# Linear attention and a gated feed-forward layer: attention of chunks 2 to 5 as 64x64 tiles of the array

## The chip, the core and the metric

The kernel runs on one core of a Trainium2 chip. The time is microseconds of the device for one execution. A core has five engines with a queue each, which run their instructions in order and wait for one another by semaphores: TensorE (PE, the matrix array of 128 rows and 128 columns, with its weight loads listed as PEld), VectorE (DVE), ScalarE (ACT), GpSimd (POOL) and SyncE (SP, used here to issue transfers). Results of PE go to PSUM, of which there are eight banks; everything else lives in SBUF.

## The reference

```python
def _attn_ref(q, k, v):                       # 4 batches, 8 heads, 768 tokens, 64 channels
    gamma = 1.0 - 2.0 ** (-5.0 - np.arange(H))
    scale = 1.0 / np.sqrt(D)
    for t in range(S):
        state = gamma[None, :, None, None] * state + np.einsum('bhd,bhe->bhde', k[:, :, t], v[:, :, t])
        y[:, :, t] = scale * np.einsum('bhd,bhde->bhe', q[:, :, t], state)
    return y
def _moe_ref(x, w_gate, w_val, w_out, rms_g): # x: 3072 tokens x 512, d_ff 1536
    rms = np.sqrt(np.mean(x * x, axis=-1, keepdims=True) + 1e-06)
    xn = x / rms * rms_g
    g = xn @ w_gate
    silu = g * (1.0 / (1.0 + np.exp(-g)))
    val = xn @ w_val
    return (silu * val @ w_out)
```

Each head keeps a decaying state of 64x64; a token adds the outer product of its key and value to it and reads it with its query. The eight heads of a token, side by side, are the 512 channels of the second function, which normalises them and runs a gated feed-forward layer. Inputs and output are float32.

## The kernel before

The 768 tokens of a batch are cut into 6 chunks (c) of 128. Inside a chunk attention is computed in the usual parallel form: scores of all pairs of the chunk's tokens, masked so that a query sees only earlier keys, times the values; to that is added what the queries read from the state as it stood before the chunk. Then the chunk's keys and values are added to the state. The decay is put into scale factors on q, k and v, so that from chunk 2 on the mask is only ones and zeros and the state is a plain sum.

The whole kernel is one list, `ORDER`, a string of some 860 words written out ahead. Each word is an operation, the indices of its chunk and batch, the PSUM banks that it uses (behind "/") and, where there is a choice, the engine (behind "@": D, A, P, S). A loop at the end of the kernel (L626 on) goes through the words and calls the function of that name; so the list sets the order of every engine's queue, the order of transfers on each queue among them. There is no other scheduler. Words that matter here, with the lines of the profile:

- `Lq`, `Lk`, `Lv` load q, k, v of a chunk and batch (L331; on POOL a transfer that also casts to bfloat16, on SP a plain one). `Cq` and `V` scale and cast q and v (L359, L378). `tq`, `tk` are transposing transfers on SP that give qT and kT (L407): two heads of 64 channels on the 128 partitions, 128 tokens, four pairs of heads (`hp`).
- `A` (L423): scores. For each pair of heads, two matmuls with 64 rows (the channels of one head) and 128 columns; the two heads stand in the two row halves of the array and write to two banks. One word does two batches.
- `M0`, `M1` (L445): the mask, on DVE, one bank of 128x512 each, from PSUM to bfloat16 in SBUF. Two for each chunk and batch.
- `Y` (L460, L464): masked scores times v, one full-array matmul of 64 columns for each head, and the read of the state, one full-array matmul of 128 columns for each pair of heads, against a block-diagonal bfloat16 copy of the state, `st_b`. For chunk 4 and half of chunk 5 the state is read by `Z` instead (L436), with 64 rows and 64 columns for one head, two batches sharing two banks, and `Y` adds only the scores' part (L455).
- `K` (L551): keys times values, 128 tokens by 64 channels on one half of the columns for each head; `U` (L560) adds the result to the float32 state `st_f` on DVE; `B` (L567) casts the state into `st_b` on POOL, two instructions for each batch.
- `S`, `R`, `N` (L474 to L505): sum of squares on ACT, 1/rms on POOL, the normalised rows on DVE. `XE` (L524): from chunk 2 on a transposing transfer on SP into `xnT`, which holds the four batches of one chunk; before that PE transposes (`X`, L518) and a copy.
- `g`, `v` (L575): gate and value matmuls, one group of 128 of the 1536 hidden channels for all 512 tokens of a chunk being four matmuls of 512 columns. `s` (L586): silu on ACT. `h` (L594): the product on DVE, into `hT`.
- `d` (L601): the output matmuls, 512 columns, twelve for each chunk and batch, in one to three words; `e` (L623) the same for the last tile in three column pieces. `o` (L141) copies to SBUF, `st` (L614) stores from SP's queue.

So a chunk's attention lies on all engines, and the feed-forward groups of the chunk before it (and the output matmuls of the one before that) are put between its steps on PE.

```python
    for w in ORDER.split():
        w, _, now["gate"] = w.partition(">")
        w, _, bk = w.partition("/")
        w, _, en = w.partition("@")
        f, *a = w.split(".")
        last[w] = F[f](ENG.get(en), [int(i) for i in bk], *map(int, a))
```

Of the kernel before, what the change touches and what calls it, by code (L numbers as in the profile page):

```python
# [9 lines left out]
F32 = mybir.dt.float32  # L10
BF16 = mybir.dt.bfloat16
# [23 lines left out]
M1.1.1 d.0.0.0.4/4 Lk.2.0@P s.0.6.7.0.4 h.0.8.9.0.4 d.0.1.0.4/1 h.0.6.7.0.4 Lk.3.1@P M0.1.0 d.0.2.0.4/2 M0.1.1
Tk.1.3/5 Tk.1.2/7 D.1.3@D Ek.1.3@A d.0.3.0.4/6 D.1.2@D Lk.2.1@P Ek.1.2@A A.1.3/53 A.1.2/70 M0.1.3 d.0.2.4.8 M1.1.3
Lk.2.2@P d.0.3.4.8 M1.1.2 Lk.2.3@P M0.1.2 d.0.1.4.8 Lk.3.0@P Y.1.2/7 K.1.1/0 S.1.2 K.1.2.2/3 U.1.1@D K.1.0/5 d.0.0.4.8
U.1.2.2@D R.1.2 U.1.0@D Y.1.0/3 B.1.2 N.1.2 Y.1.1/5 S.1.0 B.1.0 Y.1.3/0 Lq.2.3@S S.1.1 X.1.2/7 R.1.0 d.0.1.8.12
Lq.2.1@S S.1.3 Lq.2.0@S R.1.1 N.1.0 d.0.2.8.12 XE.1.2@A Lv.2.2@S o.0.1@A Lq.2.2@S R.1.3 N.1.1 X.1.0/3 Lv.2.1@S o.0.2@A
d.0.3.8.12 B.1.1 Lv.2.0@S N.1.3 XE.1.0@A X.1.1/2 B.1.3 o.0.3@D d.0.0.8.12 tk.2.2 XE.1.1@A g.1.0.1.0.3/2 o.0.0@A  # L40
v.1.0.1.0.3/6 s.1.0.1.0.3 g.1.2.3.0.3/4 h.1.0.1.0.3 v.1.1.2.0.3/2 g.1.3.4.0.3/6 tk.2.0 v.1.3.4.0.3/0 s.1.3.4.0.3
X.1.3/3 h.1.3.4.0.3 v.1.2.3.0.3/6 XE.1.3@A Cq.2.0@D g.1.1.2.0.3/0 s.1.1.2.0.3 s.1.2.3.0.3 Cq.2.3@D h.1.2.3.0.3
Cq.2.1@D v.1.10.11.0.4/3 g.1.7.8.0.4/0 g.1.10.11.0.4/6 g.1.5.6.0.4/4 g.1.9.10.0.4/5 v.1.5.6.0.4/1 v.1.9.10.0.4/7
tk.2.3 tk.2.1 tq.2.0 tq.2.1 Cq.2.2@P h.1.1.2.0.3 Lq.3.1@S Lq.3.0@S V.2.0@P tq.2.3 tq.2.2 s.1.10.11.0.4 s.1.9.10.0.4
s.1.5.6.0.4 h.1.5.6.0.4 h.1.10.11.0.4 h.1.9.10.0.4 v.1.11.12.0.4/4 g.1.6.7.0.4/1 g.1.11.12.0.4/7 g.1.8.9.0.4/3
v.1.8.9.0.4/5 v.1.7.8.0.4/6 Cq.3.1@P s.1.7.8.0.4 s.1.11.12.0.4 s.1.8.9.0.4 Cq.3.0@P h.1.11.12.0.4 h.1.7.8.0.4
h.1.8.9.0.4 A.2.0/3470 g.1.4.5.0.4/2 v.1.4.5.0.4/6 v.1.6.7.0.4/5 Lv.2.3@S tq.3.1 Lk.3.2@P s.1.6.7.0.4 s.1.4.5.0.4
M0.2.1 M1.2.1 M1.2.0 h.1.6.7.0.4 M0.2.0 V.2.1@P g.1.0.4.3.4/0 A.2.2/4271 v.1.0.4.3.4/5 Y.2.1/3 s.1.0.4.3.4 S.2.1
tk.3.1 V.2.2@P h.1.4.5.0.4 M0.2.2 M0.2.3 h.1.0.4.3.4 M1.2.3 M1.2.2 Lk.3.3@P V.2.3@P tq.3.0 R.2.1 Lv.3.1@S d.1.1.0.10/4
K.2.1/1 K.2.2.2/2 K.2.0/5 Y.2.2/7 Y.2.3/6 Y.2.0/0 d.1.1.10.12 S.2.2 S.2.3 o.1.1@A S.2.0 R.2.2 tk.3.0 N.2.1 U.2.2.2@D  # L50
U.2.0@D U.2.1@D N.2.2 XE.2.1@S R.2.0 Lq.3.3@S XE.2.2@S B.2.1 N.2.0 XE.2.0@S R.2.3 V.3.1@D N.2.3 XE.2.3@S d.1.3.0.12/1
d.1.0.0.10/7 A.3.0/6045 d.1.2.0.12/2 d.1.0.10.12 M0.3.0 M1.3.0 M1.3.1 o.1.3@D M0.3.1 st.0.0@S st.0.3@S B.2.3
v.2.6.7.0.4/1 v.2.1.2.0.4/4 g.2.3.4.0.4/5 g.2.6.7.0.4/0 g.2.1.2.0.4/6 v.2.3.4.0.4/3 Lk.4.1@P s.2.3.4.0.4 o.1.0@A
s.2.6.7.0.4 s.2.1.2.0.4 Lv.3.3@S Lq.3.2@S Cq.3.3@P B.2.0 tq.3.3 Lv.3.0@S tk.3.3 Lv.3.2@S o.1.2@D h.2.6.7.0.4
h.2.3.4.0.4 h.2.1.2.0.4 V.3.0@D Cq.3.2@P v.2.8.9.0.4/6 g.2.8.9.0.4/1 v.2.5.6.0.4/4 g.2.5.6.0.4/3 g.2.7.8.0.4/0 Y.3.0/7
g.2.2.3.0.4/5 g.2.4.5.0.4/2 Lv.4.2@S tq.3.2 Lq.4.2@S s.2.8.9.0.4 S.3.0 s.2.5.6.0.4 s.2.2.3.0.4 g.2.0.1.0.4/3
v.2.2.3.0.4/5 tk.3.2 V.3.3@P V.3.2@D h.2.8.9.0.4 h.2.5.6.0.4 h.2.2.3.0.4 st.1.3@S Lk.4.2@P Lv.4.0@S Lv.5.2@S B.2.2
R.3.0 s.2.7.8.0.4 s.2.4.5.0.4 s.2.0.1.0.4 A.3.2/2046 v.2.4.5.0.4/1 v.2.7.8.0.4/5 v.2.0.1.0.4/3 M0.3.2 M1.3.3 M1.3.2
M0.3.3 h.2.4.5.0.4 h.2.0.1.0.4 N.3.0 h.2.7.8.0.4 Lk.5.0@P Y.3.1/0 Y.3.2/4 g.2.10.11.0.4/1 Y.3.3/3 g.2.9.10.0.4/7
v.2.10.11.0.4/5 v.2.9.10.0.4/6 g.2.11.12.0.4/2 tk.4.1 Cq.4.2@P S.3.1 S.3.2 S.3.3 s.2.9.10.0.4 s.2.10.11.0.4  # L60
s.2.11.12.0.4 st.1.0@S V.4.0@P Lq.4.3@S Lq.4.1@S R.3.1 v.2.11.12.0.4/1 R.3.2 Lv.5.1@S R.3.3 N.3.2 N.3.1 N.3.3
h.2.9.10.0.4 h.2.11.12.0.4 h.2.10.11.0.4 XE.3.0@S d.2.1.0.10/2 d.2.2.0.12/5 K.3.2.2/1 K.3.0.2/6 d.2.1.10.12 Lk.4.0@P
XE.3.2@S XE.3.1@S Lv.4.3@S XE.3.3@S o.2.2@D U.3.0.2@D o.2.1@D U.3.2.2@D v.3.1.2.0.4/5 g.3.9.10.0.4/6 g.3.1.2.0.4/1
g.3.5.6.0.4/2 v.3.5.6.0.4/3 g.3.0.1.0.4/0 v.3.0.1.0.4/7 Lq.4.0@S st.0.2@S st.0.1@S Lk.4.3@P Lv.5.0@S st.1.1@S B.3.1
tk.4.2 Cq.4.3@P s.3.0.1.0.4 s.3.5.6.0.4 s.3.1.2.0.4 Lq.5.3@S h.3.0.1.0.4 h.3.1.2.0.4 Cq.4.1@D h.3.5.6.0.4
v.3.2.3.0.4/0 g.3.3.4.0.4/2 g.3.2.3.0.4/5 v.3.4.5.0.4/1 g.3.4.5.0.4/3 v.3.3.4.0.4/7 g.3.6.7.0.4/4 s.3.2.3.0.4
s.3.3.4.0.4 s.3.4.5.0.4 B.3.2 tq.4.2 V.4.3@P Lq.5.2@S V.4.2@P Cq.4.0@P tq.4.0 h.3.4.5.0.4 h.3.3.4.0.4 h.3.2.3.0.4
Lk.5.1@P tk.4.0 V.5.2@P tq.4.1 B.3.0 s.3.9.10.0.4 s.3.6.7.0.4 Lk.5.2@P Lk.5.3@P B.3.3 tq.4.3 Lv.4.1@S v.3.9.10.0.4/1
v.3.6.7.0.4/6 A.4.0/4073 Z.4.0/25 h.3.9.10.0.4 M0.4.0 h.3.6.7.0.4 Cq.5.2@D M0.4.1 M1.4.0 M1.4.1 Lq.5.0@S Lq.5.1@S
Lv.5.3@S tk.4.3 v.3.8.9.0.4/1 g.3.7.8.0.4/4 v.3.10.11.0.4/6 g.3.10.11.0.4/7 Y.4.0.2 g.3.8.9.0.4/3 d.2.3.0.12/0 V.5.1@P  # L70
# [27 lines left out]
def kernel(  # L98
# [564 lines left out]
```

## Time and profile before

| | |
|---|---|
| median of 3 runs | 231.4 us (231.13 to 231.41) |
| the profiled execution, its own time | 231.01 us |
| its span, first to last instruction or transfer | 229.0 us |
| PE busy | 222.0 us (97%), 1833 matmuls |
| PEld / DVE / ACT / POOL busy | 117.8 / 125.6 / 82.4 / 103.9 us |
| granted TensorE clock | 1.0 |
| transfers | 31.50 MB, mean 138 GB/s |

The page gives each engine's busy time, then the span in 40 slices with one digit each (9 is busy for 90% or more), then the chain of work that ended last. A group of instructions is told as line, engine, operation, tiles, shape and count, then busy time, mean length in ns, and the idle time before them with what ended it. For a matmul the shape tells the tile: 64\*128 is 64 rows by 128 columns of the array, and 64x128 behind it the channels and the columns that move through. A matmul's recorded length includes the way through the array, which the next one overlaps; and a few records can be missing.

### The profile page before, as it was taken

The page shows a single profiled execution, that of the slowest core. Times are in us where ns is not written, and L with a number is a line of the kernel's source. Part 1 is how long each engine was busy: PE and PEld are TensorE (multiplying, and loading weights), DVE is VectorE, ACT ScalarE, POOL GpSimd, SP SyncE. Part 2 cuts the span into 40 slices and gives each one's busy share as a digit, 9 for nine tenths or more (in the row PEclk, how much of TensorE's full clock was granted, in tenths as well). Part 3 has the DMA queues.
Part 4 walks back from the last instruction along what each step waited for, and adds up shares of the span by engine and source line. Part 5 has one row for each costly group of instructions (what it writes and reads, how often), then busy time and mean ns, then how long its engine had stood idle before and what let it go on. Part 6 is the DMA issues. An engine that isn't in the chain of part 4 may idle for free.

```text
span 229.0 us, 4721 instructions
## 1 busy us (share of the span) xinstructions
PE 222.0 (97%) x1833; PEld 117.8 (51%) x1859; DVE 125.6 (55%) x235; ACT 82.4 (36%) x190; POOL 103.9 (45%) x175
## 2 busy tenths in 40 slices
PE   7999999999999999999999999999999999999994
PEld 2677755565544764445544445545554444444642
DVE  6596467955636966357733585956466432163101
ACT  7897142246333240333600525400473322123031
POOL 8999999655408547345708934383130000000000
PEclk9999999999999999999999999999999999999999
DMA  7999999999859957999899997436103620010026
GB/s 146 177 174 185 185 189 190 177 167 194 181 129 157 152 95 133 213 180 283 164 179 288 127 168 155 118 71 139 47 0 69 219 82 0 0 49 0 0 94 227
DMA packets 105351, 31.50 MB, mean 138 GB/s; under 512 B 94449, under 2 KB 102385, under 8 KB 105330
## 3 DMA queue, kind: packets, MB, share of 16 engines
q0 software_dynamic: 40112, 9.70, 46.4%
q1 hardware_dynamic: 65218, 21.51, 42.7%
q8 instruction: 14, 0.23, 0.4%
q14 instruction: 7, 0.06, 0.1%
HBM read 28.31 MB, written 6.29 MB: 151 GB/s over the span
## 4 chain that ended last, share of the span: by engine, by line
PE 86%; DMA 5%; ACT 2%; issue 2%; POOL 1%; SPq 1%; DVE 1%; ACTq 0%; POOLq 0%
PE o_ps L601 25%; PE g_ps L575 25%; PE v_ps L575 24%; PE a_ps L423 3%; DMA xnT<-xn 3%; DMA qb<-in_q_dram 2%; PE y_ps L460 2%; PE kv_ps L551 1%; PE o_ps L623 1%; PE t_ps L386 1%; PE y_ps L464 1%; PE xt_ps L518 1%; SPq L524 1%; PE t_ps L391 1%; ACT sg L586 1%
## 5 line engine op out<-in xcount | busy, mean ns | idle before, releaser
L594 DVE TENSOR_TENSOR hT<-sg,v_ps 128x512 bf16<-128x512 bf16 (+2 forms) x76 | 48.1, 655 | 59.9 <-ACT sg L586 35.8
L586 ACT ACTIVATE sg<-g_ps 128x512 bf16<-128x512 f32 (+2 forms) x76 | 41.8, 575 | 102.5 <-PE g_ps L575 92.9
L575 PE MATMUL v_ps<-xnT,wv_b 128*128 128x512 bf16 (+2 forms) x338 | 70.2, 344 | 0.4
L575 PE MATMUL g_ps<-xnT,wg_b 128*128 128x512 bf16 (+2 forms) x335 | 69.4, 344 | 0.4
L601 PE MATMUL o_ps<-wo_b,hT 128*128 128x512 bf16 x265 | 61.8, 379 | 0.8 <-issue 0.3
L575 PEld LDWEIGHTS <-wv_b 128*128 128x128 bf16 x344 | 30.7, 98 | 30.3 <-issue 0.9
L575 PEld LDWEIGHTS <-wg_b 128*128 128x128 bf16 x344 | 30.3, 98 | 29.8 <-DVE hT L594 0.6
L601 PEld LDWEIGHTS <-hT 128*128 128x128 bf16 x276 | 26.2, 98 | 29.7
L445 DVE TENSOR_TENSOR am<-a_ps,causal 128x512 bf16<-128x512 f32 x32 | 20.3, 683 | 5.0 <-PE a_ps L423 5.0
L567 POOL CAST st_b<-st_f 64x256 bf16<-64x256 f32 x40 | 16.9, 422 | 9.6 <-DVE st_f L560 6.9
L331 POOL DMA_DIRECT2D kb<-in_k_dram x20 | 18.3, 915 | 2.2 <-DMA wo_b<-in_moe_w_out_dram 1.1
L359 POOL TENSOR_TENSOR qb<-qf,ydec 128x512 bf16<-128x512 f32 x10 | 10.4, 1041 | 16.8 <-DMA qf<-in_q_dram 11.3
L141 DVE COPY o_sb<-o_ps 128x512 f32<-128x512 f32 (+1 forms) x11 | 7.2, 658 | 17.5 <-DMA out_dram<-o_sb 11.7
L505 DVE SCALAR_TENSOR_TENSOR xn<-y_ps,rstd,g_bc 128x512 bf16<-128x512 f32 x18 | 13.3, 748 | 5.9 <-POOL rstd L493 5.6
L477 ACT ACTIVATE xsq<-y_ps 128x512 f32<-128x512 f32 x18 | 10.8, 600 | 15.0 <-PE y_ps L464 14.7
L378 POOL TENSOR_TENSOR vp<-vf,vdec 128x512 bf16<-128x512 f32 x12 | 12.8, 1071 | 5.1 <-DMA vf<-in_v_dram 4.8
L141 ACT COPY o_sb<-o_ps 128x512 f32<-128x512 f32 (+2 forms) x15 | 8.0, 555 | 17.1 <-PE o_ps L601 16.6
L493 POOL TENSOR_TENSOR rstd<-ms,mhalf 128x1 f32<-128x1 f32 x21 | 12.0, 572 | 1.7
L445 DVE TENSOR_TENSOR am<-a_ps,mask 128x512 bf16<-128x512 f32 x16 | 10.3, 684 | 2.3 <-PE a_ps L423 2.2
L491 POOL TENSOR_SCALAR ms<-ssq 128x1 f32<-128x1 f32 x21 | 4.3, 206 | 14.8 <-ACT xsq L477 11.4
L490 POOL TENSOR_TENSOR ssq<-ssq 128x1 f32<-128x1 f32 x6 | 1.2, 193 | 16.8 <-ACT xsq L474 16.8
L423 PE MATMUL a_ps<-qT,kT 64*128 64x128 bf16 x192 | 7.8, 217 | 0.6 <-issue 0.3
(95 smaller groups left out, 168.6 us busy)
## 6 DMA issues: line engine op xcount, KB each, us to landing
out_dram<-o_sb SPq DMA_DIRECT2D x23, 256.0 KB, 2.6
vf<-in_v_dram SPq DMA_DIRECT2D x17, 256.0 KB, 4.3
qf<-in_q_dram SPq DMA_DIRECT2D x16, 256.0 KB, 4.1
kb<-in_k_dram POOLq DMA_DIRECT2D x23, 128.0 KB, 5.6
wo_b<-in_moe_w_out_dram POOLq DMA_DIRECT2D x3, 512.0 KB, 9.3
qb<-in_q_dram POOLq DMA_DIRECT2D x8, 128.0 KB, 5.2
vp<-in_v_dram POOLq DMA_DIRECT2D x7, 128.0 KB, 8.8
wv_b<-in_moe_w_val_dram POOLq DMA_DIRECT2D x3, 256.0 KB, 6.3
```

The costliest lines, as they stand in the source:

```text
L141: return (e.copy if e is ACT else e.tensor_copy)(out, in_)
L331: i = done[n, c, b] = e.dma_start(out=x, in_=rows[n][b, c])
L378: e.tensor_tensor(out=u["vp"], in0=u["vf"], in1=vdec[:, c, :, None].to_broadcast([128, H, D]), op=ALU.mult)
L423: nc.tensor.matmul(u["a"][i][:, hp, :], u["kT"][r, hp, :], u["qT"][r, hp, :], start=True, stop=True)
L445: return DVE.tensor_tensor(out=u["am"][:, i], in0=u["a"][i], in1=m, op=ALU.mult)
L493: return POOL.tensor_tensor(out=u["rstd"], in0=ms, in1=mhalf, op=ALU.pow)
L505: return DVE.scalar_tensor_tensor(out=u["xn"], in0=flat(u["y"]), scalar=u["rstd"], in1=g_bc, op0=ALU.mult, op1=ALU.mult)
L567: POOL.tensor_copy(st_b[b][r, :, i * 64:i * 64 + 64], st_f[b // 2][r, b % 2])
L575: r = nc.tensor.matmul(p[:, (n - n0) * m:(n - n0 + 1) * m], W[w][0][:, s, n * 128:(n + 1) * 128], xnT[c][:, s, b0 * C:b1 * C], start=s == ...
L586: return ACT.activation(sg[:, :cols], done["wg", c, n0, b0][:, :cols], AF.Silu)
L594: return DVE.tensor_tensor(out=hT[c][:, n0:n1, b0 * C:b1 * C], in0=sg, in1=p, op=ALU.mult)
L601: nc.tensor.matmul(o_ps[c, b], hT[c][:, n, b * C:(b + 1) * C], wo_b[:, n, :], start=n == 0, stop=n == NFF - 1)
```

## The change

Attention of chunks 2 to 5 is written anew for a pair of batches together (g = 0: batches 0 and 1; g = 1: batches 2 and 3). The chunk is cut into two halves (s) of 64 tokens; the state is also carried from the first half to the second. All matmuls of it have 64 rows, 64 columns and 64 moving columns.

- `a`: scores inside each half alone, 32 matmuls for a pair of batches, into two banks. `m0`, `m1`: the mask, one bank of 128x512 each for two batches, with a mask of 64x64 (`causal_h`, made once by `ch`).
- `k`: keys times values of each half, 32 matmuls, one bank for each half (chunk 5: 16, the first half alone). `u0` adds the first half's bank to `st_f` and writes `st_m`; `u1` adds the second's and writes `st_f`. `b0`, `b1` cast these to bfloat16, `st_h[g][1]` and `st_h[g][0]`, 128x512 in one instruction.
- `z`: 16 of the state reads; `w`: masked scores times v (32 matmuls) and the other 16 state reads. Bank s holds the rows of half s of both batches, so that a row tile (c, 2g + s) of the feed-forward part now holds two half chunks of two batches; `st` stores it through another view of the output.
- `A`, `Z`, `M`, `Y`, `K`, `U`, `B` stay for chunks 0 and 1; the `B` words of chunk 1 become `b1`.
- The words behind the head of the list stand in a new order, with other banks, and some of the two-way choices of engine (`Cq`, `V`, `D`, `XE`, `o`) change. The count of feed-forward words is the same. The ring of the float32 k tile goes from 4 buffers to 1.

The diff, with most of the list cut:

```diff
-h.1.8.9.0.4 A.2.0/3470 g.1.4.5.0.4/2 v.1.4.5.0.4/6 v.1.6.7.0.4/5 Lv.2.3@S tq.3.1 Lk.3.2@P s.1.6.7.0.4 s.1.4.5.0.4
-M0.2.1 M1.2.1 M1.2.0 h.1.6.7.0.4 M0.2.0 V.2.1@P g.1.0.4.3.4/0 A.2.2/4271 v.1.0.4.3.4/5 Y.2.1/3 s.1.0.4.3.4 S.2.1
...
+v.1.0.1.0.3/5 k.2.0/12 tk.2.0 tk.2.1 s.1.0.1.0.3 s.1.6.7.0.4 s.1.1.2.0.3 h.1.6.7.0.4 u0.2.0 h.1.0.1.0.3 v.1.5.6.0.4/6
...
+u1.2.0 z.2.0/06 k.2.1/74 a.2.0/13 h.1.4.5.0.4 tq.2.2 Lq.3.1@S Lq.3.0@S tq.2.3 tk.2.3 m1.2.0 m0.2.0 Cq.3.0@D u0.2.1
...
+h.1.9.10.0.4 u1.2.1 h.1.11.12.0.4 w.2.0 z.2.1/15 a.2.1/72 S.2.0 S.2.1 Lv.3.0@S tk.3.1 Lv.3.1@S tk.3.0 tq.3.1 Lv.3.3@S
...
+u1.3.1 b1.3.0@A s.2.7.8.0.4 s.2.2.3.0.4 b0.3.1@A s.2.9.10.0.4 v.2.0.1.0.4/4 v.2.7.8.0.4/5 g.2.4.5.0.4/1 z.3.1/32
...
+m0.4.0 m1.4.0 h.3.9.10.0.4 u0.5.1 h.3.8.9.0.4 v.3.7.8.0.4/2 w.4.0 z.4.1/63 a.4.1/05 d.2.0.0.10/1 m0.4.1 h.3.7.8.0.4
+m1.4.1 w.4.1 d.3.1.0.10/5 d.2.0.10.12 d.3.1.10.12 d.3.0.0.10/2 d.3.3.0.12/0 d.3.0.10.12 S.4.0 S.4.1 S.4.2 S.4.3 R.4.0
...
+    HC = C // 2
+    out_h = out.rearrange("(g j c s p) m -> c g s j p m", j=2, c=S // C, s=2, p=HC)
...
-    RING = {"q": 4, "k": 4, "v": 6}
+    RING = {"q": 4, "k": 1, "v": 6}
...
+    st_m = [const.tile([128, 2, NHP, D], F32, name=f"st_m{b}") for b in range(B // 2)]
+    st_h = [[const.tile([128, 2, NHP, D], BF16, name=f"st_h{b}_{s}") for s in range(2)] for b in range(B // 2)]
+    causal_h = const.tile([128, HC], BF16, name="causal_h")
...
+    @op
+    def a(e, bk, c, g):
+        ps = pair[c, g]["a"] = [bank(bk[i], [128, 2, NHP, HC], F32, "a_ps") for i in range(2)]
+        for hp in range(NHP):
+            for j in range(2):
+                u = t[c, 2 * g + j]
+                for i in range(2):
+                    for s in range(2):
+                        nc.tensor.matmul(ps[i][half(s), j, hp, :], u["kT"][half(i), hp, half(s)],
+                                         u["qT"][half(i), hp, half(s)], start=True, stop=True)
...
+    @op
+    def k_(e, bk, c, g):
+        kv = pair[c, g]["kv"] = [bank(x, [128, 2, NHP, D], F32, "kv_ps") for x in bk]
+        for hp in range(NHP):
+            for j in range(2):
+                u = t[c, 2 * g + j]
+                for s in range(len(bk)):
+                    for i in range(2):
+                        nc.tensor.matmul(kv[s][half(i), j, hp, :], u["kb"][half(s), 2 * hp + i, :],
+                                         u["vp"][half(s), 2 * hp + i, :], start=True, stop=True)
...
+        return DVE.tensor_tensor(out=st_m[g], in0=st_f[g], in1=pair[c, g]["kv"][0], op=ALU.add)
...
+        return DVE.tensor_tensor(out=st_f[g], in0=st_m[g], in1=pair[c, g]["kv"][1], op=ALU.add)
...
+    def state(c, g, i, s, hp, start=False, stop=False):
+        for j in range(2):
+            nc.tensor.matmul(pair[c, g]["y"][s][half(j), 2 * hp + i, :], t[c, 2 * g + j]["qT"][half(i), hp, half(s)],
+                             st_h[g][s][half(i), j, hp, :], start=start, stop=stop, skip_group_check=True)
+
+    @op
+    def z(e, bk, c, g):
+        pair[c, g]["y"] = [bank(bk[s], [128, H, D], F32, "y_ps") for s in range(2)]
+        for hp in range(NHP):
+            for i in range(2):
+                state(c, g, i, 1 - i, hp, start=hp == 0)
+
+    @op
+    def w(e, bk, c, g):
+        u = pair[c, g]
+        for h in range(H):
+            for s in range(2):
+                for j in range(2):
+                    nc.tensor.matmul(u["y"][s][half(j), h, :], u["am"][half(s), h % 2, j, h // 2, :],
+                                     t[c, 2 * g + j]["vp"][half(s), h, :], start=False, stop=False, skip_group_check=True)
+        for hp in range(NHP):
+            for i in range(2):
+                state(c, g, i, i, hp, stop=hp == NHP - 1)
...
-        e.dma_start(out=out_v[c, b][:, m], in_=done["o", c, b][:, m])
+        o = out_v[c, b][:, m] if c <= 1 else out_h[c, b // 2, b % 2][:, :, m]
+        e.dma_start(out=o, in_=done["o", c, b][:, m])
```

153 lines of the change are left out of this document (88 added, 65 removed).

## The prediction

> **What bounds the kernel now.** I read the page first: busy shares, the slices, the chain of waits.
>
> ```profile
> PE 222.0 (97%) x1833; PEld 117.8 (51%) x1859; DVE 125.6 (55%) x235; ACT 82.4 (36%) x190; POOL 103.9 (45%) x175
> PE   7999999999999999999999999999999999999994
> PEclk9999999999999999999999999999999999999999
> PE 86%; DMA 5%; ACT 2%; issue 2%; POOL 1%; SPq 1%; DVE 1%; ACTq 0%; POOLq 0%
> ```
>
> TensorE is busy in every slice between the first and the last, at full granted clock, and it is 86% of the chain. A busy PE need not be a PE that never waits, so the next view is the waits of PE alone, complete:
>
> ```profile
> engine line waited for: us in total, times, longest us
> PE hot_ps L224 <- DVE one L148: 1.0, 1, 1.0
> PE t_ps L386 <- DMA qb<-in_q_dram: 0.4, 1, 0.4
> PE a_ps L423 <- issue: 0.3, 1, 0.3
> PE o_ps L601 <- issue: 0.3, 2, 0.2
> PE xt_ps L518 <- DVE xn L505: 0.2, 1, 0.2
> ```
>
> The first two rows are the head; behind it PE stands still for 0.8 us in all. So from the head to the last matmul the time is the length of the PE queue, and what the edit takes from that queue comes off the end, if the new list feeds PE as well as the old one. The other engines matter only as feeders.
>
> **What attention costs on PE now.** The groups of 70 to 170 us (by line and shape) give the counts of chunks 2 to 5:
>
> ```profile
> L423 PE MATMUL a_ps<-qT,kT 64*128 64x128 bf16 x128 | 5.0, 217 | 0.5 <-issue 0.3
> L460 PE MATMUL y_ps<-vp,am 128*128 128x64 bf16 x80 | 4.0, 193 | 0.0
> L464 PE MATMUL y_ps<-st_b,qT 128*128 128x128 bf16 x40 | 3.9, 219 | 0.0
> L551 PE MATMUL kv_ps<-vp,kb 128*64 128x64 bf16 x96 | 2.3, 198 | 0.0
> L455 PE MATMUL y_ps<-vp,am 128*128 128x64 bf16 x48 | 2.1, 193 | 0.0
> L436 PE MATMUL y_ps<-st_b,qT 64*128 64x64 bf16 x48 | 1.2, 190 | 0.0
> ```
>
> A row's busy time includes the pipeline's end behind each group, which the next group overlaps. The price of a group is therefore the time from its first start to the next group's first start, in the timeline of PE. The rate of large matmuls comes from one piece of the chain in order of time (start, length, what); the groups follow from the timeline of PE in three windows (start, length, line, names, shapes, count):
>
> ```profile
> 93.28 2.59 PE g_ps L575 x12
> ```
>
> ```profile
> 133.67 0.81 PE L575 MATMUL v_ps<-xnT,wv_b 128*128 128x512 bf16 x3
> 134.41 0.62 PE L423 MATMUL a_ps<-qT,kT 64*128 64x128 bf16 x16
> 134.87 0.40 PE L436 MATMUL y_ps<-st_b,qT 64*128 64x64 bf16 x16
> 135.20 0.60 PE L575 MATMUL v_ps<-xnT,wv_b 128*128 128x512 bf16 x2
> ...
> 118.69 0.81 PE L601 MATMUL o_ps<-wo_b,hT 128*128 128x512 bf16 x3
> 119.43 0.69 PE L551 MATMUL kv_ps<-vp,kb 128*64 128x64 bf16 x32
> 120.06 0.61 PE L601 MATMUL o_ps<-wo_b,hT 128*128 128x512 bf16 x2
> ...
> 79.81 0.71 PE L551 MATMUL kv_ps<-vp,kb 128*64 128x64 bf16 x32
> 80.45 0.41 PE L460 MATMUL y_ps<-vp,am 128*128 128x64 bf16 x8
> 80.69 0.39 PE L464 MATMUL y_ps<-st_b,qT 128*128 128x128 bf16 x4
> 80.92 0.40 PE L460 MATMUL y_ps<-vp,am 128*128 128x64 bf16 x8
> ```
>
> - Twelve large matmuls take 2.59 us: 0.216 each.
> - *Change of tile shape.* Three of them from 133.67 end at 134.32, but the first scores matmul starts at 134.41; at the update, 118.69 + 0.65 = 119.34 against 119.43. Entering a smaller shape costs about 0.09 us; I take 0.095 for each change, in or out.
> - *Scores (L423, two row tiles):* 16 in 0.46 us, 29 ns each.
> - *State read by row tiles (L436):* 16 in 0.33 less one change: 0.235, 15 ns each.
> - *Update (L551, two column tiles):* 32 in 0.63 less one change: 0.535, that is 16 pairs of 33 ns.
> - *Full array:* eight 64-wide (L460, L455) in 0.235, 29 ns each; four 128-wide (L464) in 0.23.
>
> Two tiles thus do run at once: 15 and 17 ns a matmul against 29 for the same 64 columns in the full array.
>
> Removed: 128 scores, 8 groups of 0.46, 3.7 us; 128 masked products, 16 x 0.235, 3.75; 40 full state reads, 10 x 0.23, 2.3; 48 row-tiled ones, 0.7; 96 updates, 3 x 0.535, 1.6. Together 12.05 us.
>
> **What the new attention costs.** For each chunk and pair of batches the code issues 32 matmuls in a, 32 in k (16 for chunk 5, where one bank is given), 16 in z and 48 in w; over eight such pairs 992, all 64x64 with 64 columns moving. Loops are nested so that four in a row go to four different quarters of the array, and the two row halves to different banks; in chunk 5's k only two quarters alternate. That is 240 fours and 16 pairs, 256 periods.
>
> No four-tile group is in this trace. Bounds: if a four goes as fast as a pair of row tiles (2 x 15, 29 ns), 256 x 29 = 7.4 us; if only two of four overlap, 496 periods x 33 ns = 16.4 us. I take 33 ns a four, 256 x 33 = 8.45 us, because rows split the array in one group above and columns in the other, each pair overlapping fully, and I assume that the two halvings don't hinder each other; the slower of the two periods then sets the four. The matmuls save 12.05 - 8.45 = 3.6 us.
>
> One rule speaks against this. The Trainium skill (TensorE: Matmul & The Clock Gate, "Wait — 56ns, not 53.3ns?") holds that starts of matmuls are never closer than about 25 ns, however few columns move. By it the estimate would be 992 x 25 = 24.8 us, 12.75 us more than now. Against the rule stands the row at 119.43: 32 matmuls in 0.63 us, a change of shape included, are 20 ns each.
>
> **Changes of shape.** I counted stretches in both lists. Before, scores, updates and row-tiled reads of chunks 2 to 5 make 24 changes. After, the 64x64 groups stand in 16 stretches, 32 changes, and chunk 1's update is split in two stretches, 2 more. Ten more at 0.095 is +0.95 us. A change to quarters has no row here; if it costs nothing more than the others +0.95 stands, if double, 32 x 0.095 = 3.0 us on top.
>
> **The feeders.** Rows of DVE, ACT and POOL, the landing of the transposing DMAs of L524, and of the loads of v:
>
> ```profile
> L594 DVE TENSOR_TENSOR hT<-sg,v_ps 128x512 bf16<-128x512 bf16 x64 | 42.1, 683 | 53.3 <-ACT sg L586 33.3 <-PE v_ps L575 18.5 <-remote 1.3
> L445 DVE TENSOR_TENSOR am<-a_ps,causal 128x512 bf16<-128x512 f32 x32 | 20.3, 683 | 5.0 <-PE a_ps L423 5.0
> L560 DVE TENSOR_TENSOR st_f<-st_f,kv_ps 128x512 f32<-128x512 f32 x6 | 4.1, 681 | 0.0
> L141 ACT COPY o_sb<-o_ps 128x512 f32<-128x512 f32 x13 | 7.6, 594 | 16.7 <-PE o_ps L601 16.6
> L567 POOL CAST st_b<-st_f 64x256 bf16<-64x256 f32 x40 | 16.9, 422 | 9.6 <-DVE st_f L560 6.9 <-PE y_ps L436 1.2
> DMA to landing us min/median/max: 2.4/3.1/5.1
> vf<-in_v_dram SPq DMA_DIRECT2D x17, 256.0 KB, 4.3
> ```
>
> Masks fall from 32 to 16 on DVE (-10.9 us busy); state sums rise to 14 (9.5 us), where five of this form and two half as wide stood; 32 of the 40 casts leave POOL (those behind chunks 1 to 4) for 16 copies of about 0.6 us, mostly on ACT. All of this lies beside PE and DVE is 55% busy: nothing on the path by itself. What can be late is a chain inside a chunk, where a wait also holds what stands behind it in a queue:
>
> - *k to z* now runs through u0 (0.68) and b0 (about 0.6). b0.3.1 waits on ACT with the next silu behind it. Shortest cover: three gate or value groups, 3 x 4 x 0.216 = 2.6 us against 1.3. Covered; without cover a z would cost 1.3.
> - *a to w* in chunk 4, pair 1: mask, hT product, mask on DVE, 3 x 0.683 = 2.05 us and a hand-over, behind ten output matmuls, 2.16 us. No reserve: up to 0.2.
> - *w to the gates of chunk 2:* by my count nine us of PE work cover statistics, normalising and two transposing DMAs of 3.1 us; those can take 5.1. Up to 0.3.
> - The loads of chunk 2's v move up on SP's queue ahead of the transposes; their first use, the update that stood at 79.81, moves by my count of the PE queue to about 65 us. They take 4.3 us to land and stand first among chunk 2's loads, so I cost them nothing; if late, 1 us, and the transposes of k and q behind them on SP move with them.
>
> I take +0.4 us for new waits; from -0.4 (half of today's 0.8 goes) to +3. The two small copies of the mask, the ring of k (one float tile uses it), the swapped banks and the new output address pattern (same rows, same bytes) cost nothing that reaches PE. The end is alike: then as now, a narrow matmul group, an ACT copy and a store.
>
> ```profile
> 224.64 1.15 PE L623 MATMUL o_ps<-wo_b,hT 128*128 128x192 bf16 x12
> 225.83 0.32 ACT L141 COPY o_sb<-o_ps 128x192 f32<-128x192 f32 x1 [0.41 <-PE o_ps L623]
> ```
>
> The copy ends at 226.15 and the span at 229.0; stores are queued in another order, so I allow 0.5 us either way.
>
> **Sum.** -3.6 + 0.95 + 0.4 = -2.25 us. The span goes from 229.0 to 226.75, the profiled execution from 231.01 to 228.8. The median of the runs shown, 231.4, lies 0.4 above that execution: 229.15, which I round to 229.2. A difference under 0.2%, 0.5 us, is about what a measurement here can't tell from none.
>
> **Rivals.**
>
> - *Row halves don't overlap when columns are split too* (their weights are loaded one after the other). 496 periods: 16.4 - 12.05 + 0.95 + 0.4 = +5.7, 237.1 us: slower. It decides from 47 ns a four, where matmuls save nothing (12.05 / 256); slower in all from 42. For it: no such four is in the trace. Against it: the pairs of both kinds overlap fully. 12%.
> - *Every matmul takes its own slot.* 992 x 29 = 28.8, +18.1, 249.5 us. This is the rule above in the trace's own price; the 17 ns of the update speak against it. 2%.
> - *The new list or the dearer change eats the gain:* waits of 3 us, or a double change. -3.6 + 0.95 + 3 = +0.35, 231.8 us; with both, slower by 3. For it: the chain of a chunk is one step longer and two covers have no reserve. Against: PE waits only 0.8 us today with similar covers. 16%.
> - *A four costs 29 ns and no new waits:* 7.4 - 12.05 + 0.95 = -3.7, 227.7 us. 16%.
> - The forecast, 228.3 to 230.8: 54%.
>
> Faster by over 0.2%: forecast, the 29 ns case and a little of the third, 0.73. Within: 0.07. Slower: 0.20. The range 227.3 to 232.6 leaves out the first two rivals and a little on each side.
>
> **What would show it.** Right: per four of 64x64 about 33 ns between starts; a group of a or k of 32 in about 0.27 us; changes near 0.095; PE's waits behind the head under 1.5 us; last matmul group about 2.2 us earlier. Wrong: 60 ns or more a four, or waits of PE for st_h, am or xnT of over 2 us.

## The result, and the profile after

The changed kernel takes 277.85 us (median of 4 runs, 276.36 to 279.68) against 231.26 us for the kernel before (231.07 to 231.41): a ratio of 1.202, 95% interval 1.193 to 1.211. I had forecast 229.2 us, and no rival held the result or its cause. Now and then an execution of any of these kernels takes some per cent longer, which the ranges below include and the ratios leave out.

The page of the kernel after: busy shares, slices, and two groups of copies.

```profile
span 277.9 us, 5747 instructions
PE 224.4 (81%) x2382; PEld 117.3 (42%) x2411; DVE 126.4 (45%) x232; ACT 83.8 (30%) x183; POOL 88.8 (32%) x138
PE   7999999999999999999899998998999993000000
DMA  9999999999995798999999692171000011111111
GB/s 148 168 181 150 118 181 180 197 224 156 168 172 74 181 184 183 172 214 213 110 173 184 122 54 64 32 71 50 3 0 0 21 54 51 51 51 51 50 51 37
L142 DVE COPY o_sb<-o_ps 128x512 f32<-128x512 f32 (+1 forms) x14 | 9.3, 664 | 41.8 <-DMA out_dram<-o_sb 23.1
L142 ACT COPY o_sb<-o_ps 128x512 f32<-128x512 f32 (+2 forms) x12 | 6.2, 538 | 40.4 <-DMA out_dram<-o_sb 29.1
```

The slices of PE alone tell where to look: nearly all nines as before, and then six zeros in place of none. In those last slices the row of GB/s stands at 51 and the DMA share at 1, slice after slice. Fifty is not a busy memory, since the same core moves 180 to 220 earlier; something holds the transfers to a fixed, low rate. The two groups of copies say what they are: engines that copy the output wait for earlier stores to give back `o_sb`.

The windows give the number behind the digit. Columns are the window, its length, busy time of PE, PEld, DVE, ACT and POOL, the granted clock, the DMA share and GB/s. First the kernel after, then the last busy stretch of the kernel before:

```profile
232.00:250.00 18.00, 0.00 (x0) 0.00 (x0) 1.38 (x2) 0.98 (x3) 0.00 (x0) 0.60 0.13 51
250.00:277.90 27.90, 0.00 (x0) 0.00 (x0) 0.00 (x0) 0.00 (x0) 0.00 (x0) 0.50 0.13 47
```

```profile
221.00:226.00 5.00, 4.74 (x29) 2.55 (x28) 0.69 (x1) 0.75 (x2) 0.00 (x0) 1.00 0.81 295
```

The share is a mean over 16 engines. 0.13 of 16 is about 2, the work of two engines, with fourteen standing still; before, 0.81 was 13. The records of single rows in the trace say the same without a mean: between 250 and 270 us exactly two are under way for 89% of the time and three for nearly all the rest, and a row of 2 KB takes 84 ns in the median, as in the kernel before. A store of 256 KB at 51 GB/s takes 5.1 us, and the 16 tiles of chunks 2 to 5 make 82 us of it. The issues of the stores (shortest, median, longest in ns, first and last start in us), and the timeline of the end, show the line that forms:

```profile
L705 SPq DMA_DIRECT2D out_dram<-o_sb x26: 376/789/5502, 92.7 to 265.0; - x26
```

```profile
218.06 51.88 SPq L705 DMA_DIRECT2D out_dram<-o_sb  x11
230.01 1.82 PE L714 MATMUL o_ps<-wo_b,hT 128*128 128x192 bf16 x24
...
240.41 0.98 ACT L142 COPY o_sb<-o_ps 128x512 f32<-128x512 f32 x3 [20.95 <-DMA out_dram<-o_sb]
...
245.54 0.69 DVE L142 COPY o_sb<-o_ps 128x512 f32<-128x512 f32 x1 [9.56 <-DMA out_dram<-o_sb]
```

PE ends at 230.01 + 1.82 = 231.83; the last copy only at 246.2, and SP issues stores until 270. The two remaining rows of the comparison are where the feed-forward part begins, before and after:

```profile
16.56 0.51 PE L575 MATMUL g_ps<-xnT,wg_b 128*128 128x128 bf16 x6
```

```profile
21.02 1.07 PE L665 MATMUL g_ps<-xnT,wg_b 128*128 128x128 bf16 x16
```

So the 48.9 us between the two spans (229.0 and 277.9) split in three: the head +4.46 (21.02 against 16.56), PE's queue from there to its end +1.58 (210.81 against 225.79 - 16.56 = 209.23), and what lies behind PE +42.86 (46.07 against 3.21). The head's part is of this one execution, in which groups of the first 17 us took 1.5 to 1.9 times as long as in the first experiment below (why isn't known: the granted clock reads 1.0 in both); there the same list reaches that group at 17.06 us. PE's waits behind the head in the kernel after:

```profile
PE g_ps L665 <- DMA xnT<-xn: 1.2, 1, 1.2
PE o_ps L691 <- issue: 1.0, 6, 0.2
PE kv_ps L485 <- DMA kb<-in_k_dram: 0.7, 1, 0.7
PE a_ps L462 <- DVE hT L684: 0.7, 1, 0.7
```

Transposing transfers stand on SP's queue among the slow stores. The last one for `xnT`, issued at 182.31 us behind a store, landed 7.7 us later, where those of the kernel before took 2.4 to 5.1. So part of the loss reaches PE too.

### The profile page after: what moved, and what is told of

Its sections match the earlier page's. It is cut to its first block, busy times and chain, and to the rows that moved or that the text cites. A ratio compares the mean times of both kernels' runs of the same rounds, so it can differ in the third digit from the quotient of the medians.

```text
span 277.9 us, 5747 instructions
## 1 busy us (share of the span) xinstructions
PE 224.4 (81%) x2382; PEld 117.3 (42%) x2411; DVE 126.4 (45%) x232; ACT 83.8 (30%) x183; POOL 88.8 (32%) x138
## 4 chain that ended last, share of the span: by engine, by line
PE 53%; DMA 20%; issue 5%; POOL 4%; SPq 4%; DVE 2%; ACT 1%; DVEq 0%; POOLq 0%; ACTq 0%
PE v_ps L665 16%; PE g_ps L665 15%; PE o_ps L691 11%; DMA out_dram<-o_sb 10%; DMA kb<-in_k_dram 4%; SPq L705 3%; DMA xnT<-xn 3%; DMA qb<-in_q_dram 2%; DMA vf<-in_v_dram 2%; POOL kb L336 1%; PE t_ps L391 1%; POOL vp L383 1%; PE a_ps L428 1%; PE hot_ps L229 1%; PE y_ps L522 1%
## 5 line engine op out<-in xcount | busy, mean ns | idle before, releaser
L665 PE MATMUL g_ps<-xnT,wg_b 128*128 128x512 bf16 (+2 forms) x336 | 69.1, 344 | 1.8 <-DMA xnT<-xn 1.2
L665 PE MATMUL v_ps<-xnT,wv_b 128*128 128x512 bf16 (+2 forms) x334 | 69.3, 343 | 0.9 <-issue 0.5
L691 PE MATMUL o_ps<-wo_b,hT 128*128 128x512 bf16 x265 | 61.9, 379 | 1.2 <-issue 1.0
L665 PEld LDWEIGHTS <-wg_b 128*128 128x128 bf16 x344 | 30.5, 98 | 32.4 <-issue 1.7
L665 PEld LDWEIGHTS <-wv_b 128*128 128x128 bf16 x344 | 30.4, 98 | 29.3 <-DVE hT L684 0.3
L691 PEld LDWEIGHTS <-hT 128*128 128x128 bf16 x276 | 26.0, 98 | 29.8 <-DVE xn L595 0.4
L142 DVE COPY o_sb<-o_ps 128x512 f32<-128x512 f32 (+1 forms) x14 | 9.3, 664 | 41.8 <-DMA out_dram<-o_sb 23.1
L595 DVE SCALAR_TENSOR_TENSOR xn<-y_ps,rstd,g_bc 128x512 bf16<-128x512 f32 x24 | 17.7, 748 | 9.6 <-POOL rstd L583 9.6
L567 ACT ACTIVATE xsq<-y_ps 128x512 f32<-128x512 f32 x24 | 14.2, 597 | 22.8 <-PE y_ps L506 17.3
L142 ACT COPY o_sb<-o_ps 128x512 f32<-128x512 f32 (+2 forms) x12 | 6.2, 538 | 40.4 <-DMA out_dram<-o_sb 29.1
L364 POOL TENSOR_TENSOR qb<-qf,ydec 128x512 bf16<-128x512 f32 x9 | 9.4, 1042 | 14.2 <-DMA qf<-in_q_dram 14.2
L471 DVE TENSOR_TENSOR am<-a_ps,causal_h 128x512 bf16<-128x512 f32 x16 | 10.6, 685 | 4.5 <-PE a_ps L462 3.6
L383 POOL TENSOR_TENSOR vp<-vf,vdec 128x512 bf16<-128x512 f32 x7 | 7.3, 1043 | 8.8 <-DMA vf<-in_v_dram 8.8
L229 PE MATMUL hot_ps<-one 128*128 128x512 bf16 x17 | 7.5, 573 | 1.0 <-DVE one L149 1.0
L142 POOL CAST st_h<-st_m 128x512 bf16<-128x512 f32 x3 | 2.2, 742 | 18.3 <-DVE st_m L490 18.3
L364 DVE TENSOR_TENSOR qb<-qf,ydec 128x512 bf16<-128x512 f32 x7 | 4.8, 685 | 5.1 <-DMA qf<-in_q_dram 5.1
```

Source lines behind the costliest of these rows:

```text
L142: return (e.copy if e is ACT else e.tensor_copy)(out, in_)
L364: e.tensor_tensor(out=u["qb"], in0=u["qf"], in1=ydec[:, c, :, None].to_broadcast([128, H, D]), op=ALU.mult)
L471: return DVE.tensor_tensor(out=x, in0=y, in1=causal_h[:, None, :].to_broadcast([128, 2 * NHP, HC]), op=ALU.mult)
L567: return ACT.activation(xsq, flat(u["y"]), AF.Square, accum_out=u["ssq"])
L595: return DVE.scalar_tensor_tensor(out=u["xn"], in0=flat(u["y"]), scalar=u["rstd"], in1=g_bc, op0=ALU.mult, op1=ALU.mult)
L665: r = nc.tensor.matmul(p[:, (n - n0) * m:(n - n0 + 1) * m], W[w][0][:, s, n * 128:(n + 1) * 128], xnT[c][:, s, b0 * C:b1 * C], start=s == ...
```

## The experiments

**Theory.** The view `out_h[...]` of a store has the shape 2, 64, columns, where `out_v` has 128, columns. Same rows and bytes, but the outermost count is 2, and only that many engines carry it. **Rivals.** The address order itself (two blocks of rows 768 apart) is slow at the memory; or the other half of the edit (64x64 tiles, new list) delays the copies and the stores with them.

### The change without its store

```diff
-        o = out_v[c, b][:, m] if c <= 1 else out_h[c, b // 2, b % 2][:, :, m]
-        e.dma_start(out=o, in_=done["o", c, b][:, m])
+        e.dma_start(out=out_v[c, b][:, m], in_=done["o", c, b][:, m])
```

> The changed kernel with one line undone: every store goes through the old view of the output, 128 rows in a row (so the rows of chunks 2 to 5 land in other places of the output than the reference has them). Theory 1, the store's new view has an outermost dimension of 2, so two of the sixteen DMA engines carry a whole store, 64 rows of 84 ns each = 5.4 us, and the end is the backlog of these stores: the tail behind PE shrinks from 46 us to about 3, time 229 to 233 us. Theory 2, the new list overloads SP's queue and the stores are late whatever their view: stays above 270 us.

Measured: 228.89 us (228.57 to 230.05), against 231.57 for the kernel before on that chip: 0.9897 (0.9866 to 0.9927). Its PE groups, first and last, and its longest waits behind the warm-up:

```profile
17.06 0.51 PE L665 MATMUL g_ps<-xnT,wg_b 128*128 128x128 bf16 x6
...
222.41 1.82 PE L713 MATMUL o_ps<-wo_b,hT 128*128 128x192 bf16 x24
```

```profile
PE o_ps L691 <- issue: 1.0, 6, 0.2
PE t_ps L391 <- DMA qb<-in_q_dram: 0.8, 1, 0.8
PE v_ps L665 <- issue: 0.5, 3, 0.2
```

PE's queue from the first gate group is 224.23 - 17.06 = 207.17 us, 2.06 less than before, and the waits for `xnT`, `kb` and `hT` are gone. So the edit without that one view makes the kernel about 1% faster; the view costs 49 us.

### The kernel before, with the new store alone

```diff
-        e.dma_start(out=out_v[c, b][:, m], in_=done["o", c, b][:, m])
+        o = out_v[c, b][:, m] if c <= 1 else out_h[c, b // 2, b % 2][:, :, m]
+        e.dma_start(out=o, in_=done["o", c, b][:, m])
```

> The kernel before with only the stores of chunks 2 to 5 sent through the new two-piece view (their rows land in other places than the reference has them). Theory 1: 16 stores of 5.4 us on two engines, 51 GB/s, 86 us of stores in one line; the end moves to 260 to 280 us though attention and list are the old ones. Theory 2 (the list): 231 us.

Measured: 275.58 us (one run). Its windows and PE's waits:

```profile
264.00:270.00 6.00, 0.00 (x0) 0.00 (x0) 0.00 (x0) 0.00 (x0) 0.00 (x0) 0.50 0.13 51
```

```profile
PE v_ps L577 <- DMA xnT<-xn: 7.8, 1, 7.8
PE a_ps L425 <- DVE hT L596: 2.6, 1, 2.6
```

A changed view in the old kernel adds 44 us (231.57 to 275.58), with the same 0.13 and the same 51 GB/s, with old tiles and old list. That rules out the second rival. The first row of waits shows the second way by which slow stores cost time: PE waited 7.8 us for a transposing transfer that stood behind them on SP.

### Four pieces and sixteen in place of two

Is it the address order, or the count? Two kernels ask that, both the kernel before with another view:

```diff
+    out_q = out.rearrange("(b c s p) m -> c s b p m", b=B, s=4, p=C // 4)
-        e.dma_start(out=out_v[c, b][:, m], in_=done["o", c, b][:, m])
+        o = out_v[c, b][:, m] if c <= 1 else out_q[c, b][:, :, m]
+        e.dma_start(out=o, in_=done["o", c, b][:, m])
```

> The kernel before with the stores of chunks 2 to 5 through a view of four pieces of 32 rows, one in each batch (rows land in other places than the reference has them). Theory 1, as many engines as pieces: four engines, about 102 GB/s, 2.7 us a store; the eight stores of chunks 4 and 5 need 22 us and the end comes at about 236 to 245 us, between before and the two-piece store. Theory 3 (places far apart): as slow as two pieces or slower, 260 us or more.

```diff
+    out_s = out.rearrange("(a t p) m -> t a p m", a=16, p=8)
-        e.dma_start(out=out_v[c, b][:, m], in_=done["o", c, b][:, m])
+        e.dma_start(out=out_s[4 * c + b][:, :, m], in_=done["o", c, b][:, m])
```

> The kernel before, all stores through a view of sixteen pieces of 8 rows, 192 rows apart (rows land in other places than the reference has them). Theory 1, as many engines as pieces: sixteen engines, no loss, 231 to 232 us. Theory 3 (scattered places cost): slower than with four pieces, over 253 us.

Measured: four pieces 253.48 us, sixteen 233.57 us (one run each). A stretch with stores under way, first of four pieces, then of sixteen:

```profile
234.00:238.00 4.00, 0.00 (x0) 0.00 (x0) 0.69 (x1) 0.00 (x0) 0.00 (x0) 0.81 0.26 102
```

```profile
222.00:228.00 6.00, 5.07 (x31) 2.69 (x29) 0.69 (x1) 1.14 (x3) 0.00 (x0) 1.00 0.72 217
```

0.26 of 16 is 4.2, at twice the rate of two pieces; 0.72 is 11.5. In the records of single rows four are under way for 82% of 234 to 246 us, and with sixteen pieces 16 is the commonest count; a row takes 84 ns in the median in both. The count of pieces sets the engines, and sixteen pieces, the most scattered addresses of the three, take 2.0 us more than rows in one run (233.57 against 231.53), not 44: it is not the address order. The 231 to 232 us that I had expected of them were 1.6 too few; one run can't tell whether that is a cost. The Trainium skill (DMA: Bandwidth & Descriptors, "Why a DMA increments its semaphore by 16 and not by 1") states this rule: the count of engines is the largest number up to 16 that divides the slowest dimension, other than 1, of both access patterns; its "Rules for kernel authors" add that an outermost size below 16 confines the whole transfer to at most that many engines. The first two shares, about 2 and 4.2, agree with it; 11.5 is above 8, so it fits the 16 that the rule gives, with gaps between the stores.

My size for four pieces was too low (253 where at most 245 was expected). I had worked it out from the stores' backlog alone; but PE itself ends 7.4 us later than in the kernel before (233.24 against 225.79), 4.1 of it in waits for `xnT`:

```profile
PE v_ps L576 <- DMA xnT<-xn: 4.1, 2, 3.9
```

### Mending it: two stores of 64 rows

To keep the right places and the 16 engines, each store becomes two, from two halves of the partitions:

```diff
-        o = out_v[c, b][:, m] if c <= 1 else out_h[c, b // 2, b % 2][:, :, m]
-        e.dma_start(out=o, in_=done["o", c, b][:, m])
+        if c <= 1:
+            e.dma_start(out=out_v[c, b][:, m], in_=done["o", c, b][:, m])
+            return
+        for j in range(2):
+            e.dma_start(out=out_h[c, b // 2, b % 2][j, :, m], in_=done["o", c, b][half(j), m])
```

> The changed kernel with each store of chunks 2 to 5 cut into two, one for each batch, 64 rows in a row each, to the same places. Theory 1 (too few engines for a view with an outermost dimension of 2): as fast as with all rows in a row, 229 to 233 us, plus at most 0.5 us for 16 more issues at the end. Theory 3 (writes to two places far apart are slow in themselves): stays above 270 us.

Measured: 233.66 us (233.41 to 238.99), 1.0097 (1.0071 to 1.0124) against before: 44 us back, yet 1% slower than the kernel before, 4.8 us above the first experiment and just over the range expected. PE ends at 223.97 here, as early as in the first experiment (224.23); the rest is SP. Its issues of stores, its timeline, and the window behind PE:

```profile
L708 SPq DMA_DIRECT2D out_dram<-o_sb x36: 467/594/1554, 124.5 to 228.7; - x36
```

```profile
220.48 8.78 SPq L708 DMA_DIRECT2D out_dram<-o_sb  x14
```

```profile
224.00:231.60 7.60, 0.00 (x0) 0.00 (x0) 0.00 (x0) 0.27 (x1) 0.00 (x0) 0.76 0.45 108
```

From 209.02 us SP has 26 stores to issue. It waits twice for copies on the way, and from 220.48 to 229.26 (220.48 + 8.78) it issues the last 14, one behind the other without a gap; the span ends 2.3 us later. The list leaves most stores of chunks 3 to 5 to the very end; with one DMA for each they just fit, with two they don't.

### The same two stores in the kernel before

```diff
+        if c <= 1:
+            e.dma_start(out=out_v[c, b][:, m], in_=done["o", c, b][:, m])
+            return
+        for j in range(2):
+            r = slice(j * 64, j * 64 + 64)
+            e.dma_start(out=out_v[c, b][r, m], in_=done["o", c, b][r, m])
-        e.dma_start(out=out_v[c, b][:, m], in_=done["o", c, b][:, m])
```

> The kernel before, each store of chunks 2 to 5 cut into two of 64 rows to the same places. Theory 1a: twice ten issues of 0.6 us from 221 us on, and a last landing of 3 us: 235 to 237 us, so that the price of half stores needs nothing of the new attention. If the price comes with the two places far apart: 231.4 us.

Measured: 238.03 us (one run), 1 us above the expectation, with no 64x64 tile in it. Issues of its stores, and for comparison those of the kernel before unchanged and with sixteen pieces:

```profile
L619 SPq DMA_DIRECT2D out_dram<-o_sb x36: 466/595/1864, 156.8 to 233.0; - x36
```

```profile
L614 SPq DMA_DIRECT2D out_dram<-o_sb x26: 332/450/1243, 88.7 to 226.2; - x26
```

```profile
L615 SPq DMA_DIRECT2D out_dram<-o_sb x26: 538/586/1377, 89.4 to 227.9; - x26
```

An issue takes 0.60 us for half the rows, 0.59 in sixteen pieces and 0.45 for 128 rows in a run. So splitting a store doubles the issues and makes each dearer. In both kernels with half stores the line of issues is what ends last: from the end of its last issue to the end of the span it is 2.3 us with two stores and 2.5 here, as in the kernel before (2.5), so the landing adds nothing, although half stores are slower in the DMA engines too (last section).

### Taking the issues off the end

Three stores (of chunks 2 and 3) that stood at the very end go to where SP has time, and each last store comes behind its own copy; then the second half of each store of chunks 4 and 5 goes to ACT's queue; then the last copy goes from ACT to DVE. Each edit is shown against the kernel ahead of it, the first against the one with two stores, and lines of the list are shortened to the words that change:

```diff
-XE.5.1@S st.3.0@S s.4.5.6.0.4
+XE.5.1@S st.3.0@S st.3.3@S st.2.2@S st.3.2@S s.4.5.6.0.4
...
-st.4.1@S st.3.3@S st.2.2@S e.5.3.1/5
+st.4.1@S e.5.3.1/5
...
-o.5.3.1@D o.5.2@D o.5.0@D o.4.2@A o.5.3.0@A o.5.3.2@A o.5.1@D
-st.4.2@S st.5.0@S st.5.2@S st.5.3.1@S st.3.2@S st.5.1@S st.5.3.0@S st.5.3.2@S
+o.4.2@A st.4.2@S o.5.3.1@D st.5.3.1@S o.5.2@D st.5.2@S o.5.0@D
+st.5.0@S o.5.1@D st.5.1@S o.5.3.0@A st.5.3.0@S o.5.3.2@A st.5.3.2@S
```

> The changed kernel with two stores of 64 rows for a tile, and the store words moved in the list: the stores of tiles 3.3, 2.2 and 3.2, whose data lie ready long before, from the end to behind the store of 3.0, and the last seven in the order in which PE finishes their tiles. Theory 1a: what two stores still lose against one (4.8 us) is SP's issue queue, 26 issues of about 0.6 us behind 209 us; six issues fewer are 3.6 us, time 229.5 to 231 us. If the half stores lose the time in flight and not at the issue: no more than 1 us gained, 232.5 us or more.

```diff
-            e.dma_start(out=out_h[c, b // 2, b % 2][j, :, m], in_=done["o", c, b][half(j), m])
+            q = ACT if c >= 4 and j else e
+            q.dma_start(out=out_h[c, b // 2, b % 2][j, :, m], in_=done["o", c, b][half(j), m])
```

> The one before, and the second half of each store of chunks 4 and 5 issued from ACT's queue, which has nothing else to do by then. Theory 1a (issue on SP): the issues at the end are halved, 228.5 to 229.5 us, as fast as the kernel with all rows in a row. If the DMA engines carry half stores at half speed whoever issues them: the same as with the stores only moved.

```diff
-o.5.3.2@A
+o.5.3.2@D
```

> The kernel with two queues, with the copy of the last column piece on DVE instead of ACT, where it stood behind the issue of a store (0.5 us). If the tail is that queue: the last stores leave 0.3 to 0.5 us sooner, 229.8 to 230.0 us. If the tail is only the landing of the last store: no change, 230.2 us.

Measured: 231.09 us (230.61 to 232.04) for the moved stores, 0.9987 (0.9971 to 1.0003); with two queues 230.25, 0.9938 (0.9918 to 0.9959), both against 231.53 on that chip; with the copy on DVE 229.86 (229.51 to 231.22) against 231.84, 0.9926 (0.9898 to 0.9955). The first is at the upper end of what was expected, the second missed it: 228.5 to 229.5 us, as fast as with all rows in a row, were forecast. The third came as forecast, but its interval overlaps that of the second, so what the copy is worth isn't settled. By its median the last one is the fastest of all kernels here that put every row at its place. The ends of SP's line with moved stores, and of both queues with two (the last store still waits for a copy on ACT, which has its own issues between):

```profile
L708 SPq DMA_DIRECT2D out_dram<-o_sb x36: 466/594/1258, 125.2 to 226.3; - x36
```

```profile
220.59 4.78 SPq L709 DMA_DIRECT2D out_dram<-o_sb  x4
...
224.07 0.50 ACTq L709 DMA_DIRECT2D out_dram<-o_sb  x1
...
224.61 0.27 ACT L142 COPY o_sb<-o_ps 128x128 f32<-128x128 f32 x1 [0.57 <-PE o_ps L718]
...
224.91 0.54 ACTq L709 DMA_DIRECT2D out_dram<-o_sb  x1
```

The last issue goes from 228.7 (two stores as they stood) to 226.3 to 224.9, and the time follows it: 233.66, 231.09, 230.25.

### Do the quarters of the array owe their pace to the nesting of the loops?

My first rival had been that the two row halves don't overlap. In the kernel with two queues (its copy still on ACT), the loops are now nested so that all matmuls of one row half come first and the neighbours in the list are column pairs only:

```diff
-        for hp in range(NHP):
-            for j in range(2):
-                u = t[c, 2 * g + j]
-                for s in range(len(bk)):
+        for s in range(len(bk)):
+            for hp in range(NHP):
+                for j in range(2):
+                    u = t[c, 2 * g + j]
```

(so in `k`; likewise `i` or `s` outermost in `a`, `z`, `w`)

> The kernel with two queues, with the loops of a, k, z and w nested the other way: all matmuls of one row half first, then all of the other, so that only two column tiles alternate. The same matmuls, the same banks. If a period of about 32 ns holds one matmul for each quarter that is in use, 240 fours become 480 pairs: PE's queue grows by 7.6 us, time 237 to 238 us, and groups of 32 take 0.5 us instead of 0.25. If each 64x64 matmul costs its 8 ns whatever stands beside it: 230.3 us, as before the edit.

Measured: 232.73 us (231.96 to 234.4), 1.0049 (1.0005 to 1.0092) against 231.84. PE's queue from the first gate group is 209.27 us long (17.73 to 227.00), 2.3 more than with two queues and the old nesting (17.08 to 224.08, 207.0): neither nothing nor the 7.6 of no overlap. A `k` that stands alone, and a place where `a` follows `k`:

```profile
66.81 0.60 PE L485 MATMUL kv_ps<-vp,kb 64*64 64x64 bf16 x32
67.34 1.04 PE L665 MATMUL v_ps<-xnT,wv_b 128*128 128x512 bf16 x4
...
73.42 0.48 PE L485 MATMUL kv_ps<-vp,kb 64*64 64x64 bf16 x26
73.71 0.22 PE L462 MATMUL a_ps<-qT,kT 64*64 64x64 bf16 x2
73.73 0.20 PE L485 MATMUL kv_ps<-vp,kb 64*64 64x64 bf16 x2
73.76 0.19 PE L462 MATMUL a_ps<-qT,kT 64*64 64x64 bf16 x1
73.77 0.19 PE L485 MATMUL kv_ps<-vp,kb 64*64 64x64 bf16 x1
```

The lone group takes 0.53 less a change of 0.095, 0.435, where by column pairs alone it would be 16 x 33 = 0.53 and the same group in fours took 0.285 (in the first experiment; its rows stand in the next section). In the other place starts of L462 lie between starts of L485, although the list has all of `k` ahead of `a`: matmuls of the one row half begin before earlier ones of the other half have begun. By the rows only a few run ahead so, so the nesting is worth part of the overlap, not all; how far it reaches wasn't measured.

## Why the prediction was wrong

**What PE has to do: right.** The argument was that PE's queue is the length and the edit shortens it by 2.25 us. With the store's view taken back it is 2.06 us shorter, and the time is 228.89 us for 229.2 forecast, with the bulk of the change in place. The groups of that kernel on PE's timeline:

```profile
66.14 0.45 PE L485 MATMUL kv_ps<-vp,kb 64*64 64x64 bf16 x32
66.52 1.04 PE L665 MATMUL v_ps<-xnT,wv_b 128*128 128x512 bf16 x3
...
71.71 0.81 PE L665 MATMUL v_ps<-xnT,wv_b 128*128 128x512 bf16 x3
72.45 0.32 PE L506 MATMUL y_ps<-st_h,qT 64*64 64x64 bf16 x16
72.60 0.43 PE L485 MATMUL kv_ps<-vp,kb 64*64 64x64 bf16 x32
72.85 0.52 PE L462 MATMUL a_ps<-qT,kT 64*64 64x64 bf16 x32
73.30 0.40 PE L665 MATMUL g_ps<-xnT,wg_b 128*128 128x128 bf16 x4
```

- *Fours at 33 ns:* 32 updates (L485) from 72.60 to 72.85 are 31 ns a four. The 32 scores behind them (L462) take 0.45 less a change back to the full array, 0.355 or 44 ns a four; why they are slower wasn't looked for. The Trainium skill's 25 ns between starts (TensorE: Matmul & The Clock Gate, "Wait — 56ns, not 53.3ns?"), held at 2%, doesn't hold across quarters of the array: 32 starts in 0.25 us are 7.8 ns apart. For matmuls on one and the same tile no run here tests it.
- *Changes at 0.095:* three large matmuls from 71.71 take 0.65, to 72.36; the first quarter starts at 72.45. 0.09: a change to quarters costs what the others do, and the doubled price didn't come.
- *Waits +0.4:* `k` to `z`, `a` to `w`, `w` to the gates, the loads of `v`: none is among the waits of that kernel, whose longest behind the head is 0.2 us. Covered, as worked out, so the 0.4 was too much. The 1.7 us called issue in its list are no lost time: its trace lacks 29 records of large matmuls (it has 265 of 276 in L691 and 670 of 688 in L665), while the kernel with two queues, whose trace has all of them, shows 0.4 us of waits behind the first transposes in a queue of 207.0 us.
- *The sum, partly by luck:* in that kernel's trace the 16 stretches of 64x64 groups take 10.7 us up to the matmul behind each; less 16 changes at 0.095 that is 9.2 us, where 8.45 were forecast. So the fours were some 0.7 us dearer, the scores most plainly, and the waits that did not come made up for part of it.
- *The head* came 0.50 us later in that execution (17.06 for 16.56), which I had not looked at; it takes a quarter of PE's gain away, and together with the stretch behind PE (2.97 for 3.21 us) it makes the span 227.2 where I had 226.75.

**The output's addresses: wrong, and all of the result.** The step that failed is "the new output address pattern (same rows, same bytes) cost nothing that reaches PE", with "The end is alike: then as now, a narrow matmul group, an ACT copy and a store", for which I allowed 0.5 us either way. I had priced the transfer by its bytes and rows and never by the shape of its view. In its place the runs showed: two engines for each store of chunks 2 to 5 (share 0.13, 51 GB/s), 5.1 us each, a line of stores that is 46 us long when PE is done; with that view alone the old kernel goes from 231.57 to 275.58, without it the new one from 277.85 to 228.89. The bound could have been had from the profile of before: 295 GB/s at a share of 0.81 is 23 GB/s for each engine, so a store on two engines gets 46 GB/s, 5.7 us for 256 KB, 91 us for 16 of them. What was missing was the question of how many engines a view of 2, 64 is given. That trace doesn't answer it, but a bound for few engines could have stood in the sum, and I gave none.

**The rivals: all about PE.** Row halves that don't overlap, a slot for each matmul, waits on the list: none came. "Some transfer that the edit rewrites gets slower" wasn't among them, though the diff's last two lines rewrite one.

**What stays open.** The two stores of 64 rows don't give back all: 229.86 us at best, against 228.89 with one store for each tile (whose rows land elsewhere). The ratios to the kernel before, 0.9926 and 0.9897, have intervals that overlap, so the size of the rest is not settled. Whether one store with 128 rows outermost on both sides and a 64-row jump inside could have both wasn't tried. Nor was the cause of the pace of half stores, below, looked for.

## What to carry to other kernels

When an edit rewrites the address side of a transfer, look at the view's outermost count before its bytes: multiply the DMA share of a stretch by 16 to get the engines at work; an even 0.13 was two here. Price each transfer that the diff touches by itself, with a bound for fewer engines, and its issue on the queue as well, since transfers and later work on that queue wait behind it. And list the rivals by the lines of the diff, not by the engine that one thinks is the bound.

## What the runs showed of the hardware that I had not expected

- Two engines carry a store in two pieces at 24.5 GB/s each (51 / 2.08, 84 ns for a row of 2 KB). In the two stores of 64 rows from SP alone an engine has a much lower pace. The kernel before with half stores, two windows at its end:

```profile
224.00:230.00 6.00, 3.05 (x22) 1.76 (x20) 0.69 (x1) 0.91 (x2) 0.00 (x0) 1.00 0.75 174
230.00:236.00 6.00, 0.00 (x0) 0.00 (x0) 0.00 (x0) 0.00 (x0) 0.00 (x0) 0.61 0.48 111
```

174 GB/s at 0.75 of 16 engines is 14.5 GB/s for each, and 111 at 0.48 the same: 141 ns for a row of 2 KB. Full stores at the end of the kernel before had 22.8 (295 at 0.81). In the kernel with two queues, the records of single rows behind 211 us give 151 ns in the median for the half stores from SP and 84 for those from ACT. SP has the first half of each store there and ACT the second; but with both halves on SP (two stores as they stood) fewer than a quarter of the last rows are that fast, so the half alone doesn't explain it. The cause stays open.

- A change from the full array to quarters of it costs 0.09 us, no more than to halves.
- Matmuls of one row half of the array start ahead of earlier ones of the other half (rows of L462 and L485 above), so four-way overlap needs neighbours in the list less strictly than I had assumed.
